# Linear attention, then two MLPs, on one core: the order of the first eight steps and of the loads ahead of them

## The chip, the cores and the metric

The kernel runs on 1 core of one Trainium2 chip. The metric is device microseconds of one execution, the median of the runs. A core has TensorE (PE), VectorE (DVE), ScalarE (ACT), GpSimd (POOL) and SyncE (SP), which issues nearly all of the DMAs here. PE, DVE and ACT work through their instructions in the order in which they were written out; so does SP with its DMAs.

## The reference

```python
# attention without softmax: 8 batches, 8 heads, 576 tokens, 64 per head
kv = np.einsum('bhsd,bhse->bhde', k, v)
out = np.einsum('bhsd,bhde->bhse', q, kv)
rms = np.sqrt(np.mean(out * out, axis=-1, keepdims=True) + 1e-06)
attn = out / rms * g_norm
x = attn.transpose(0, 2, 1, 3).reshape(4608, 512)
# first MLP, 512 -> 2048 -> 512
h = x @ w_in
x = (h * np.cos(h)) @ w_out
# second MLP, 512 -> 1024 -> 1024 -> 512
a = x @ w1
b = x @ w2
out = (a * b @ w3) @ w_out2
```

## The kernel before

**Tiles and stages.** The 4608 tokens are cut in nine blocks of 512 for the first MLP, and its 2048 inner columns in sixteen pieces m of 128. One step is one pair (block, m). A step makes h (12 matmuls of 128x512: four chunks of the 512 inputs, each as three products of a high and a low half, `three`, L756), then g = h cos h, and two steps later adds g times a piece of w_out to the four banks of x2 (`emit_w`, L786, 12 matmuls). The eight steps 0 to 7 (`HM` is 8) are block 0 with m 0 to 7; then block 1 runs with all sixteen m, and only then the second half of block 0. The second MLP (L990) takes the rest of the span.

**Words.** The weights arrive as 64-bit words and are converted on the chip, one tile of 128x512 at a time (`Chunk`, L118). A conversion is one pass of ACT (L141) and four of DVE (L142 to L149); then `put` makes the high half on ACT (L112) and the low half on DVE (L114). Tiles i0, i1, ... are w_in of piece 0, 1, ..., tiles u0, u1, ... are w_out; they come in the order i0 i1 i2 u0 i3 u1 and so on. `prefetch(n)` issues loads up to tile n, `begin` starts one conversion, `each` makes one further DVE pass on the conversions in hand.

**Attention.** A batch has two units (halves of its tokens) and four pairs of heads p. For a pair: 20 small matmuls make kv (`emit_kv`, L264; the last four read `kvrest`, the tail of the tokens), ACT copies the two 64x64 blocks (`copy_kv`, L459), PE multiplies q of the two units by them (`emit_whole`, L465), ACT squares the result (`emit_square`, L475) and keeps it times the norm's weight (`emit_keep`, L481), and PE sums the squares (`emit_sums`, L484, six small matmuls a unit). When all pairs are summed, `norms` (L493) makes 1/rms in eleven short DVE instructions, PE spreads it over the rows (`emit_rows`, L497), and DVE multiplies the kept result by it. `split_x` (L736) makes the high and the low half of x for a block.

**The first batches.** Block 0 is units 0 and 1, all of batch 0, made in `first_batch` (L511) ahead of step 0. Units 2 and 3 (batch 1) are made inside the steps 0 to 7, in `first_steps` (L571). From step 8 on a scheduler orders the work; in `first_batch` and `first_steps` the order on PE, DVE and ACT is the order of the code. `load_first` (L407) gives the order of SP's loads in the head. A load goes out when one of eight earlier ones has landed, and for a word tile also when its buffer has been converted.

**What ties the engines.** h has two PSUM banks: h of a step needs the product with the cosine (L642) of the step two back. g has two buffers: ACT's high half of g (L112) waits until x2 of two steps back has read its buffer. The banks "pa" are two; kv of a pair, the outputs of units 2 and 3 and their spread rows take turns in them. In the steps' output banks the squares' sums have a corner of their own, so a pair's q matmul must wait until ACT has kept the pair before.

**One step of `first_steps` before.** In the code's order: h of step n; squares and sums of pair p = n - 2; x2 of step n - 2; ACT's r and DVE's first u (L632, L633, called the phase here); DVE passes; the sine (L637); product (L642); split of g; keep of pair p; q matmuls of pair n - 1; more passes, then `put`. Norms come at the end of step 5, rows in steps 6 and 7.

Of the kernel before, what the change touches and what calls it, by code (L numbers as in the profile page):

```python
# [33 lines left out]
def kernel(  # L34
# [18 lines left out]
    nc = tc.nc  # L53
# [353 lines left out]
    def load_first():  # L407
# [32 lines left out]
        kv(0, 1, nc.sync)  # L440
        prefetch(1)
        kv(0, 2, nc.sync)
        qs(0, 2, nc.sync)
        prefetch(2)
        kv(0, 3, nc.sync)
        qs(0, 3, nc.sync)
        prefetch(6)
        rest(1, nc.sync)
        kv(1, 0, nc.sync)
        kv(1, 1, nc.sync)  # L450
        prefetch(8)
        for p in range(NPAIR):
            if p >= 2:
                kv(1, p, nc.sync)
            qs(1, p, nc.sync)

    whole = []
# [53 lines left out]
    def first_batch(spread, x, y, t):  # L511

        sums = ps_h.tile([P, 512], F32, tag="h", name="ms_first")
        units = range(NHALF)
        count = [1, 1, 2, 2]

        def pieces(n):
            made = [c.convert() for c in chunks[state["conv"]:state["conv"] + n]]
# [13 lines left out]
        for p in range(NPAIR):  # L532
            for u in units:
                emit_whole(u, p, ps_acc.tile(
                    [P, 512], F32, tag=f"acc{(2 * p + u) % 4}", name=f"out_{u}_{p}"
                )[:, 0:HALF])
            for u in units:
                emit_square(u, p)
            if p == 0:
                made = pieces(count[0])  # L540
            rest_of(made)
            if p > 0:
                put(count[p - 1])
            if p + 1 < NPAIR:
                emit_kv(0, p + 1)
                copy_kv(p + 1)
            if p == 0:
                nc.scalar.activation(gneg, gneg, AF.Copy, scale=-1.0)
            for u in units:
                emit_sums(u, p, sums, fresh=True)  # L550
            for u in units:
                emit_keep(u, p)
            if p + 1 < NPAIR:
                made = pieces(count[p + 1])
        for p in range(2):
            emit_kv(1, p)
        norms(sums, x, y, t)
        put(count[-1])
        for p in range(2):
            copy_kv(p)  # L560
        for p in range(NPAIR + 1):
            if p < NPAIR:
                for u in units:
                    ps = ps_acc.tile(
                        [P, 512], F32, tag=f"acc{(2 * p + u) % 4}", name=f"spread_{u}_{p}"
                    )
                    mm = emit_rows(u, p, ps, y, spread)
            if p > 0:
                split_x(0, p - 1)

    def first_steps(spread, x, y, t):  # L571
# [29 lines left out]

        prefetch(min(state["put"] + 8, n_first))
        pair = [begin(), begin()]
        for n in range(HM):
            p = n - 2
            last = n == HM - 1
            emit_h(n)
            if n == 1:
                for k in (2, 3):
                    emit_kv(1, k)  # L610
                    copy_kv(k)
                for v in units:
                    out_bank(v, 0)
            if 0 <= p < NPAIR:
                for v in units:
                    emit_square(v, p)
                sums = banks[units[0]][:, HALF:HALF + NR]
                for v in units:
                    emit_sums(v, p, sums)
            if n == NPAIR + 2:  # L620
                rows(0)
            if n >= 2:
                emit_w(n - 2)
            if n == 0:
                for _ in range(3):
                    each()
            if last:
                scale(1)
                rows(2)
# [8 lines left out]
            if last:  # L638
                for c in range(2):
                    split_x(1, c)  # L640
            new = [begin()] if n < HM - 2 else []
            nc.vector.tensor_tensor(u, u, h_ps.pop(n), ALU.mult)  # L642
            if n > 0:
                each()
            if last:
                scale(2)
                rows(3)
            g_hl[n] = m1.tile([P, 2, TB], F32R, tag="g", bufs=2, name=f"g_{n}")
            since.extend([h_last.pop(n), *split(g_hl[n], u, nc.vector)])
            new += [begin()] if n < HM - 2 else []  # L650
            if 0 <= p < NPAIR:
                for v in units:
                    emit_keep(v, p)
            if 1 < n <= NPAIR:
                for v in units:
                    out_bank(v, n - 1)
            if n == NPAIR + 2:
                scale(0)
                rows(1)
# [4 lines left out]
            if n == NPAIR + 1:  # L664
                norms(sums, x, y, t)
        split_x(1, 2)
        scale(3)
        made = split_x(1, 3)
# [714 lines left out]
```

## Time and profile before

| | us |
|---|---|
| median of 3 runs | 1538.41 |
| lowest, highest | 1533.98, 1540.04 |
| the profiled execution | 1537.59 |
| its span, first to last instruction | 1535.5 |
| PE busy in the span | 1490.5 |
| DVE, ACT, POOL busy | 866.8, 675.0, 349.3 |

The profile's times are those of the profiled execution, counted from its first instruction. A matmul's busy time overlaps that of the next one, so a stretch in which PE is fully busy says that there was always a matmul under way, not how fast it went; the granted clock beside it says whether the clock was at its upper level (1.00) or the lower one (0.50). A wait is shown in brackets behind the instruction that waited, with what ended it.

### The profile page before, as it was taken

Reading aid. Unit: us, or ns where it says so; the run is one execution under the profiler, and the core shown is the slowest. Engines: PE = TensorE matmul, PEld = TensorE weight load, DVE = VectorE, ACT = ScalarE, POOL = GpSimd, SP = SyncE. Lnnn points to the kernel's source line nnn. Section 1 sums busy time; section 2 is a strip of 40 time slices with the busy share of each in tenths; the row PEclk is TensorE's granted clock in tenths of the full one; section 3 lists DMA queues with packets and bytes.
Section 4 is the critical chain, followed back from the end, with each engine's and each line's share of the span. In section 5 each row is a group of like instructions: output and inputs, shape, how many; then the busy total and the mean of one; then the engine's idle time right before and its main releaser. Section 6 shows DMA issues by size and latency. Waiting matters only on the chain.

```text
span 1535.5 us, 20577 instructions
## 1 busy us (share of the span) xinstructions
PE 1490.5 (97%) x7728; PEld 1273.7 (83%) x7728; DVE 866.8 (56%) x1558; ACT 675.0 (44%) x1356; POOL 349.3 (23%) x278
## 2 busy tenths in 40 slices
PE   5879999999999999999999998999999999999998
PEld 4667888888788887888888887999999988999997
DVE  4777854456465665656555436755545546445543
ACT  4545654444445454444534335444433334333331
POOL 0000011010010111101102005455344237344330
PEclk7989999999999999999999999999999999999999
DMA  9325231433424435244222106122112313233312
GB/s 361 126 69 156 69 90 41 148 88 110 126 78 132 130 100 149 85 123 132 85 74 80 41 8 226 42 69 69 53 58 83 110 48 110 74 112 124 124 62 76
DMA packets 81299, 155.02 MB, mean 101 GB/s; under 512 B 11232, under 2 KB 36944, under 8 KB 81200
## 3 DMA queue, kind: packets, MB, share of 16 engines
q1 hardware_dynamic: 80224, 152.08, 30.4%
q8 instruction: 60, 0.98, 0.3%
q0 software_dynamic: 272, 1.05, 0.2%
q10 hardware_dynamic: 704, 0.59, 0.1%
q14 instruction: 39, 0.32, 0.1%
HBM read 112.57 MB, written 41.12 MB: 100 GB/s over the span
## 4 chain that ended last, share of the span: by engine, by line
PE 91%; DMA 3%; DVE 2%; ACT 1%; POOL 1%; issue 1%; SPq 0%; ACTq 0%; DVEq 0%
PE X L990 13%; PE x L757 9%; PE x L758 9%; PE h L757 9%; PE x L759 8%; PE h L758 8%; PE h L759 8%; PE V L990 6%; PE o L758 4%; PE o L757 4%; PE o L759 4%; PE Y L990 3%; PE kv L277 2%; DMA q<-in_qt_dram 1%; DMA u_w<-in_w1pair_dram 1%
## 5 line engine op out<-in xcount | busy, mean ns | idle before, releaser
L990 PE MATMUL X<-xc,w 128*128 128x384 f32 x1152 | 226.3, 337 | 4.5 <-DVE wchl L114 2.3
L758 PE MATMUL x<-g,w_out 128*128 128x512 f32 x576 | 225.3, 391 | 0.0
L759 PE MATMUL x<-g,w_out 128*128 128x512 f32 x576 | 224.7, 390 | 0.0
L757 PE MATMUL x<-g,w_out 128*128 128x512 f32 x576 | 223.2, 394 | 0.0
L776 DVE SCALAR_TENSOR_TENSOR u<-h,r 128x512 f32<-128x512 f32 x136 | 93.9, 691 | 216.7 <-ACT r L774 212.0
L757 PE MATMUL h<-x,w_in 128*128 128x512 f32 x544 | 215.6, 397 | 0.0
L990 PEld LDWEIGHTS X<-xc,w 128*128 128x128 f32 x1152 | 204.3, 189 | 12.0 <-ACT s L998 3.2
L758 PE MATMUL h<-x,w_in 128*128 128x512 f32 x544 | 213.2, 392 | 0.2 <-DVE x L114 0.2
L759 PE MATMUL h<-x,w_in 128*128 128x512 f32 x544 | 212.9, 391 | 0.0
L114 POOL TENSOR_TENSOR xc<-x2r,xc 128x768 fp32r<-128x768 f32 x70 | 135.1, 1940 | 228.6 <-ACT xc L112 228.6
L774 ACT ACTIVATE r<-h 128x512 int32<-128x512 f32 x136 | 81.1, 597 | 212.7 <-PE h L759 203.2
L114 POOL TENSOR_TENSOR qhl<-q,qhl 128x288 fp32r<-128x288 f32 x48 | 40.1, 835 | 469.9 <-ACT qhl L112 469.9
L112 ACT ACTIVATE g<-u 128x512 fp32r<-128x512 f32 x144 | 91.0, 632 | 126.9 <-DVE u L781 84.5
L114 DVE TENSOR_TENSOR g<-u,g 128x512 fp32r<-128x512 f32 x144 | 102.9, 714 | 63.1 <-ACT g L112 62.9
L998 ACT ACTIVATE s<-X 128x384 f32<-128x384 f32 x144 | 66.6, 488 | 152.5 <-PE X L990 151.9
L757 PEld LDWEIGHTS x<-g,w_out 128*128 128x128 f32 x576 | 108.5, 188 | 23.3 <-issue 0.2
L759 PEld LDWEIGHTS x<-g,w_out 128*128 128x128 f32 x576 | 108.4, 188 | 22.7
L758 PEld LDWEIGHTS x<-g,w_out 128*128 128x128 f32 x576 | 108.6, 189 | 22.0
L757 PEld LDWEIGHTS h<-x,w_in 128*128 128x128 f32 x544 | 102.8, 189 | 25.4 <-DVE u L781 3.3
L759 PEld LDWEIGHTS h<-x,w_in 128*128 128x128 f32 x544 | 102.7, 189 | 21.4
L758 PEld LDWEIGHTS h<-x,w_in 128*128 128x128 f32 x544 | 102.7, 189 | 21.0 <-DVE x L114 0.6
L781 DVE TENSOR_TENSOR u<-u,h 128x512 f32<-128x512 f32 x136 | 93.0, 684 | 47.4 <-ACT u L780 47.3
(177 smaller groups left out, 2479.2 us busy)
## 6 DMA issues: line engine op xcount, KB each, us to landing
x2r<-x_all SPq DMA_DIRECT2D x44, 384.0 KB
kvraw<-in_kv_main_dram SPq DMA_DIRECT2D x32, 512.0 KB
x_all<-x2s SPq DMA_DIRECT2D x36, 256.0 KB
part<-o SPq DMA_DIRECT2D x36, 256.0 KB
part<-part SPq DMA_DIRECT2D x36, 256.0 KB
out_dram<-part SPq DMA_DIRECT2D x36, 256.0 KB
i_w<-in_w1pair_dram SPq DMA_DIRECT2D x16, 512.0 KB
u_w<-in_w1pair_dram SPq DMA_DIRECT2D x16, 512.0 KB
```

The lines of the kernel that those rows point to most:

```text
L112: hi = nc.scalar.activation(dst[:, 0], src, AF.Copy)
L114: lo = lo_engine.tensor_tensor(dst[:, 1], src, f32(dst[:, 0]), ALU.subtract)
L277: nc.tensor.matmul(ps[d], k[:, d], v[:, d], start=fresh and i == 0, stop=i == NC, skip_group_check=True,)
L757: nc.tensor.matmul(ps, w[0], x[0], start=first, stop=False)
L758: nc.tensor.matmul(ps, w[0], x[1], start=False, stop=False)
L759: return nc.tensor.matmul(ps, w[1], x[0], start=False, stop=last).ins
L774: nc.scalar.activation(r, h_ps[n], AF.Identity, bias=0.25, scale=INV_2PI)
L776: nc.vector.scalar_tensor_tensor(u, h_ps[n], INV_2PI, r, ALU.mult, ALU.subtract)
L781: nc.vector.tensor_tensor(u, u, h_ps.pop(n), ALU.mult)
L990: nc.tensor.matmul(ps, w[:, self.i, a, k], x[:, b, k], start=first and k == 0 and n == 0, stop=last and k == 1 and n == 2, skip_group_chec ...
L998: copied.append(nc.scalar.activation(s, ps, AF.Copy).ins)
```

## The change

In `load_first` the word tiles come sooner: tile 1 ahead of q of pair 2, tile 2 behind it, tile 3 behind the fourth kv, all eight ahead of the second batch's tail; and the second batch's four kv loads stand ahead of its q loads in the code. (On SP the second batch's loads come out in nearly the same order as before, its tail of the tokens still last but for one q load.)

In `first_batch` the conversions are taken 1, 1, 1, 1 and 2 at a time, so that the fourth tile is converted behind the third. The kv matmuls of the second batch's pairs 0 and 1 and their copies are no longer there.

On PE, at the end of `first_batch`, there stood before (ms_first is the sum of squares, kv_1 the second batch, spread the rows of 1/rms):

```order
L488 MATMUL ms_first_168<-sel_86,sq_1_3_312 96x2 x3
L277 MATMUL kv_1_0_336<-kvraw_1_0_146 64x64 x8
L277 MATMUL kv_1_0_336<-kvrest_1_144 64x64 x2
L277 MATMUL kv_1_1_347<-kvraw_1_1_148 64x64 x8
L277 MATMUL kv_1_1_347<-kvrest_1_144 64x64 x2
L501 MATMUL spread_0_0_379<-rs_first_99 64x96 x6
L501 MATMUL spread_1_0_387<-rs_first_99 64x96 x6
```

and now:

```order
L487 MATMUL ms_first_168<-sel_86,sq_0_3_310 96x2 x3
L487 MATMUL ms_first_168<-sel_86,sq_1_3_312 96x2 x3
L500 MATMUL spread_0_0_353<-rs_first_99 64x96 x6
L500 MATMUL spread_1_0_361<-rs_first_99 64x96 x6
L500 MATMUL spread_0_1_369<-rs_first_99 64x96 x6
```

The kv groups have gone behind h of step 1, where those of pairs 2 and 3 already were; the copies of pairs 2 and 3 stay behind the first `put` of the steps.

In `first_steps` a step now runs as: x2 of step n - 2; h of step n + 1; r, phase, passes, sine; squares of pair n - 1; product, split of g; sums and keep of pair n - 1; q matmuls of pair n; last passes and `put`. So h of a step is made a step sooner, and the attention pairs run one step sooner too. On ACT, step 2 stood so before (sq squares, o keep, r and u the step's phase and sine, i and u with _f word tiles):

```order
L479 ACTIVATE sq_2_0_610<-out_2_561 128x288
L479 ACTIVATE sq_3_0_613<-out_3_563 128x288
L632 ACTIVATE r_2_637<-h_2_596 128x512
L637 ACTIVATE u_2_638<-u_2_638 128x512
L141 ACTIVATE i7_f_646<-i7_w_470 128x512
L112 ACTIVATE g_2_651<-u_2_638 128x512
L141 ACTIVATE u5_f_654<-u5_w_472 128x512
L482 ACTIVATE o_2_609<-out_2_561,gneg_87 128x288
L482 ACTIVATE o_3_612<-out_3_563,gneg_87 128x288
```

and stands so now:

```order
L627 ACTIVATE r_2_654<-h_2_565 128x512
L632 ACTIVATE u_2_655<-u_2_655 128x512
L478 ACTIVATE sq_2_1_663<-out_2_561 128x288
L478 ACTIVATE sq_3_1_665<-out_3_563 128x288
L141 ACTIVATE i7_f_667<-i7_w_444 128x512
L112 ACTIVATE g_2_672<-u_2_655 128x512
L481 ACTIVATE o_2_587<-out_2_561,gneg_87 128x288
L481 ACTIVATE o_3_590<-out_3_563,gneg_87 128x288
L141 ACTIVATE u5_f_685<-u5_w_446 128x512
```

The squares are of pair 1 instead of pair 0 and stand behind the sine; the keep stands ahead of the second word tile's pass.

The norms of units 2 and 3 stay in step 5, now ahead of the low halves of that step's `put`, with the rows of pair 0 directly behind them; rows of pair 1 stand between x2 of step 4 and h of step 7, rows 2 behind h of step 7, rows 3 behind x2 of step 5. Step 6 converts one word tile instead of two; the other one (u8) is converted ahead of step 8's phase. From step 8 on the scheduler makes another order. On PE the end of h of step 9 and x2 of step 7 were apart:

```order
L757 MATMUL h_9_1101<-x_1_1013,w_in1_278 128x512
L758 MATMUL h_9_1101<-x_1_1013,w_in1_278 128x512
L759 MATMUL h_9_1101<-x_1_1013,w_in1_278 128x512
L757 MATMUL x2_0_0_621<-g_7_1043,w_out7_873 128x512
L758 MATMUL x2_0_0_621<-g_7_1043,w_out7_873 128x512
L759 MATMUL x2_0_0_621<-g_7_1043,w_out7_873 128x512
```

and are now mixed with h of step 8:

```order
L766 MATMUL x2_0_0_625<-g_7_1032,w_out7_909 128x512
L766 MATMUL x2_0_1_629<-g_7_1032,w_out7_909 128x512
L766 MATMUL x2_0_2_633<-g_7_1032,w_out7_909 128x512
L766 MATMUL h_8_1068<-x_1_1018,w_in0_234 128x512
L766 MATMUL h_9_1101<-x_1_1018,w_in1_272 128x512
L767 MATMUL x2_0_0_625<-g_7_1032,w_out7_909 128x512
L768 MATMUL x2_0_0_625<-g_7_1032,w_out7_909 128x512
L767 MATMUL h_8_1068<-x_1_1018,w_in0_234 128x512
```

The second halves of h of both steps moved back, in among x2 of step 7. Further back PE has the same instructions in the same order but for some small moves in steps 10 to 18.

The diff, cut to its core:

```diff
         kv(0, 2, nc.sync)
+        prefetch(2)
         qs(0, 2, nc.sync)
-        prefetch(2)
+        prefetch(3)
         kv(0, 3, nc.sync)
+        prefetch(4)
         qs(0, 3, nc.sync)
-        prefetch(6)
+        prefetch(8)
         rest(1, nc.sync)
...
-        count = [1, 1, 2, 2]
+        count = [1, 1, 1, 1, 2]
...
+            if p == 2:
+                rest_of(pieces(count[3]))
             if p + 1 < NPAIR:
-                made = pieces(count[p + 1])
-        for p in range(2):
-            emit_kv(1, p)
+                made = pieces(count[p + 1 if p < 2 else 4])
         norms(sums, x, y, t)
         put(count[-1])
-        for p in range(2):
-            copy_kv(p)
...
+        emit_h(0)
+        emit_h(1)
         for n in range(HM):
-            p = n - 2
-            last = n == HM - 1
-            emit_h(n)
+            p = n - 1
+            begins = 2 if n < 5 else 1 if n == 5 else 0
...
             if n >= 2:
                 emit_w(n - 2)
+            if n == 6:
+                scale(0)
+                rows(1)
+            if 1 <= n < HM - 1:
+                emit_h(n + 1)
...
+            if 0 <= p < NPAIR:
+                for v in units:
+                    emit_square(v, p)
...
+            if n == 0:
+                for k in range(NPAIR):
+                    emit_kv(1, k)
+                    if k < 2:
+                        copy_kv(k)
             if 0 <= p < NPAIR:
+                sums = banks[units[0]][:, HALF:HALF + NR]
+                for v in units:
+                    emit_sums(v, p, sums)
                 for v in units:
                     emit_keep(v, p)
+                if p + 1 < NPAIR:
+                    for v in units:
+                        out_bank(v, p + 1)
...
+            if n == 5:
+                norms(sums, x, y, t)
+                rows(0)
             put(len(pair))
+            if n == 0:
+                for k in (2, 3):
+                    copy_kv(k)
+            if n == 6:
+                scale(1)
+                rows(2)
```

## Rows read from the trace of the kernel before

**Rows 1.** The page, engines: busy us, share of the span, instructions.

```profile
PE 1490.5 (97%) x7728; PEld 1273.7 (83%) x7728; DVE 866.8 (56%) x1558; ACT 675.0 (44%) x1356; POOL 349.3 (23%) x278
```

**Rows 2.** Busy time by stretch: length; PE, PEld, DVE, ACT, POOL; clock; DMA share; GB/s.

```profile
27.50:38.00 10.50, 1.84 (x26) 1.51 (x24) 5.05 (x16) 1.61 (x4) 0.00 (x0) 0.50 1.04 396
...
56.00:99.00 43.00, 34.84 (x170) 27.35 (x168) 34.79 (x65) 26.49 (x52) 0.00 (x0) 0.96 0.32 112
...
125.00:180.00 55.00, 55.00 (x271) 44.45 (x270) 45.08 (x83) 30.43 (x55) 0.81 (x1) 1.00 0.37 115
180.00:1535.00 1355.00, 1344.53 (x6801) 1156.37 (x6799) 737.90 (x1293) 583.30 (x1165) 343.85 (x260) 1.00 0.29 93
```

**Rows 3.** The chain that ended last, from 16 us: start, us, what.

```profile
27.93 8.20 DMA kvrest<-in_kv_tail_dram
```

**Rows 4.** Timeline, 27 to 44 us: start, us, instruction, [idle before <- what ended it].

```profile
29.14 0.20 DVE L494 TENSOR_SCALAR rs_first<-ms_first 96x48 f32<-96x48 f32 x1
...
36.17 0.48 PE L277 MATMUL kv<-kvrest 64*64 64x64 f32 x4 [8.66 <-DMA kvrest<-in_kv_tail_dram]
...
38.03 6.11 PE L501 MATMUL spread<-rs_first 96*64 96x96 f32 x96
```

**Rows 5.** Timeline, 8 to 19 us: loads on SP, a word tile's first passes.

```profile
8.79 0.33 SPq L413 DMA_DIRECT2D kvraw<-in_kv_main_dram  x1
...
10.60 0.33 SPq L132 DMA_DIRECT2D i_w<-in_w1pair_dram  x1
...
18.20 0.67 ACT L141 ACTIVATE i_f<-i_w 128x512 f32<-128x512 f32 x1 [0.39 <-DMA i_w<-in_w1pair_dram]
18.90 0.43 DVE L142 TENSOR_SCALAR i_f<-i_f 128x512 f32<-128x512 f32 x1 [0.48 <-ACT i_f L141]
```

**Rows 6.** Timeline, 50 to 57 us: from kv of the second batch to step 1.

```profile
50.27 0.69 PE L277 MATMUL kv<-kvraw 128*64 128x64 f32 x16
...
55.05 1.66 PE L467 MATMUL out<-q,rs_first 128*128 128x288 f32 x4 [2.95 <-ACT rs_first L463]
...
56.12 0.69 DVE L633 SCALAR_TENSOR_TENSOR u<-h,r 128x512 f32<-128x512 f32 x1 [0.74 <-ACT r L632]
```

**Rows 7.** Timeline, 62 to 74 us: step 2 on DVE, ACT and PE, step 3's phase.

```profile
63.54 0.69 DVE L633 SCALAR_TENSOR_TENSOR u<-h,r 128x512 f32<-128x512 f32 x1 [0.39 <-ACT r L632]
...
70.14 0.69 DVE L114 TENSOR_TENSOR w_out<-u_f,w_out 128x512 fp32r<-128x512 f32 x1
73.17 0.69 DVE L633 SCALAR_TENSOR_TENSOR u<-h,r 128x512 f32<-128x512 f32 x1 [2.34 <-ACT r L632]
...
66.88 0.63 ACT L112 ACTIVATE g<-u 128x512 fp32r<-128x512 f32 x1 [1.42 <-PE x L759]
...
67.96 0.87 ACT L482 ACTIVATE o<-out,gneg 128x288 f32<-128x288 f32 x2
...
68.50 1.24 PE L467 MATMUL out<-q,rs_first 128*128 128x288 f32 x4 [1.66 <-ACT o L482]
72.34 1.10 PE L488 MATMUL out<-sel,sq 128*96 128x2 f32 x12
```

**Rows 8.** Timeline, 99 to 125 us: norms of units 2 and 3, rows, step 8.

```profile
99.14 0.20 DVE L494 TENSOR_SCALAR rs_first<-out 96x48 f32<-96x48 f32 x1
...
101.85 2.19 PE L501 MATMUL spread<-rs_first 96*64 96x96 f32 x24 [3.90 <-DVE rs_first L370]
...
110.26 2.15 PE L501 MATMUL spread<-rs_first 96*64 96x96 f32 x24 [1.90 <-DVE o L600]
...
120.99 1.21 PE L501 MATMUL spread<-rs_first 96*64 96x96 f32 x24 [1.13 <-DVE o L600]
122.13 0.50 PE L757 MATMUL x<-g,w_out 128*128 128x512 f32 x1
...
124.98 0.39 PE L757 MATMUL h<-x,w_in 128*128 128x512 f32 x1
```

**Rows 9.** Timeline, 115 to 150 us: step 8's phase on DVE.

```profile
128.82 0.69 DVE L776 SCALAR_TENSOR_TENSOR u<-h,r 128x512 f32<-128x512 f32 x1 [3.89 <-ACT r L774]
```

More of the change, by code (lines that the diff above doesn't have):

```diff
@@ L442, in load_first @@
         kv(0, 2, nc.sync)
+        prefetch(2)
         qs(0, 2, nc.sync)
-        prefetch(2)
+        prefetch(3)
         kv(0, 3, nc.sync)
+        prefetch(4)
         qs(0, 3, nc.sync)
-        prefetch(6)
+        prefetch(8)
         rest(1, nc.sync)
-        kv(1, 0, nc.sync)
-        kv(1, 1, nc.sync)
-        prefetch(8)
         for p in range(NPAIR):
-            if p >= 2:
-                kv(1, p, nc.sync)
+            kv(1, p, nc.sync)
+        for p in range(NPAIR):
             qs(1, p, nc.sync)
@@ L542, in first_batch @@
             if p > 0:
-                put(count[p - 1])
+                put(count[p - 1] if p < 3 else 2)
             if p + 1 < NPAIR:
@@ L566, in first_batch @@
                     )
-                    mm = emit_rows(u, p, ps, y, spread)
+                    emit_rows(u, p, ps, y, spread)
             if p > 0:
@@ L603, in first_steps @@
         pair = [begin(), begin()]
+        emit_h(0)
+        emit_h(1)
         for n in range(HM):
-            p = n - 2
-            last = n == HM - 1
-            emit_h(n)
+            p = n - 1
+            begins = 2 if n < 5 else 1 if n == 5 else 0
+            new = []
             if n == 1:
-                for k in (2, 3):
-                    emit_kv(1, k)
-                    copy_kv(k)
                 for v in units:
                     out_bank(v, 0)
[L614 to L621, printed above, removed]
             if n >= 2:
                 emit_w(n - 2)
+            if n == 6:
[3 more added lines that the diff above has]
+                emit_h(n + 1)
             if n == 0:
@@ L626, in first_steps @@
                     each()
-            if last:
-                scale(1)
-                rows(2)
+            if n == HM - 1:
+                scale(2)
+                rows(3)
             r = stage([P, TB], I32, f"r_{n}")
@@ L637, in first_steps @@
             nc.scalar.activation(u, u, AF.Sin, bias=HALF_PI, scale=TWO_PI)
-            if last:
+            if n == HM - 1:
                 for c in range(2):
                     split_x(1, c)
-            new = [begin()] if n < HM - 2 else []
+            if 0 <= p < NPAIR:
+                for v in units:
+                    emit_square(v, p)
+            if begins > 0:
+                new.append(begin())
             nc.vector.tensor_tensor(u, u, h_ps.pop(n), ALU.mult)
@@ L644, in first_steps @@
                 each()
-            if last:
-                scale(2)
-                rows(3)
             g_hl[n] = m1.tile([P, 2, TB], F32R, tag="g", bufs=2, name=f"g_{n}")
             since.extend([h_last.pop(n), *split(g_hl[n], u, nc.vector)])
-            new += [begin()] if n < HM - 2 else []
+            if n == 0:
[3 more added lines that the diff above has]
+                        copy_kv(k)
             if 0 <= p < NPAIR:
+                sums = banks[units[0]][:, HALF:HALF + NR]
+                for v in units:
+                    emit_sums(v, p, sums)
                 for v in units:
                     emit_keep(v, p)
[L654 to L659, printed above, removed]
+                if p + 1 < NPAIR:
+                    for v in units:
+                        out_bank(v, p + 1)
+            if begins > 1:
+                new.append(begin())
             each()
+            if n == 5:
+                norms(sums, x, y, t)
+                rows(0)
             put(len(pair))
+            if n == 0:
[4 more added lines that the diff above has]
+                rows(2)
             pair = new
             prefetch(min(state["put"] + 8, n_first))
-            if n == NPAIR + 1:
-                norms(sums, x, y, t)
         split_x(1, 2)
```

## The prediction

> **What bounds the kernel now.** The page's table of engines was read first: TensorE (PE) is busy for 97% of the span [rows 1]. So a change pays only where it takes idle or slow time out of PE. The busy time by stretch shows where that is [rows 2]: from 125 to 180 us PE is busy 55.00 of 55, and from 180 to 1535 us it is busy 1344.53 of 1355. From 125 us on the kernel is PE's own work, at granted clock 1.00, and it starts when the first eight steps are over. Ahead of that PE is idle for some 34 us: 8.66 of the 10.5 from 27.5 to 38, and 8.2 of the 43 from 56 to 99, where VectorE (DVE) is busy 34.79 and so doesn't fill the time either. The change touches only this head. The mark for it is the first matmul of step 8, at 124.98 us [rows 8]: what it moves forward, the end moves forward, as long as nothing behind it becomes later than PE.
>
> Three things hold the head. First, one load: PE waits 8.66 us for the tail of the second batch's kv, which lands at 36.1, 8.2 us after it was issued [rows 3, 4]. The norms of the first batch start at 29.14 and need none of it, but their spread matmuls stand behind it, at 38.03. Second, the steps: step 2's phase on DVE starts at 63.54 and the next at 73.17, 9.63 us later, though DVE's last instruction of the step starts at 70.14. It then waits 2.34 for ScalarE's r, which waits for h on PE. ScalarE (ACT) in its turn waits 1.42 for PE's x, because g has two buffers, and PE waits 1.66 for ACT's copy of the attention output [rows 7]. So the three engines hand one step round, one after the other. Third, the norms of units 2 and 3: PE waits 3.90, then 1.90 and 1.13 for rows and scales [rows 8].
>
> **The first batch.** The four kv matmul groups go behind the second h. Spread then follows the norms. From the norms' first instruction to the first spread matmul it takes 2.71 us in the second batch (99.14 to 101.85 [rows 8]), so from 29.14 the spread would start at 31.85, not 38.03: 6.2 us. There is some more. DVE converts words without a break from 18.90 to 29.14, and that run begins with a word tile for which ACT had waited until 18.20 [rows 5]. This tile was issued at 10.60. In the new queue it takes the place of the load at 8.79, 1.8 us sooner. Of these 1.8 I take 0.8, since the fourth tile's first pass is now behind a copy on ACT. What it passes on SP's queue goes back: the fourth kv load by that one slot, q of pair 3 by two word tiles. Their readers on PE stand behind the squares' sums, so I cost that at nothing; uncovered it would take back some 0.4. First term: **7.0**, ends 5.8 (no sooner word, a late kv load) and 8.0 (all 1.8).
>
> The Trainium skill, DMA: Bandwidth & Descriptors, section Specifications, gives about 358 GB/s as what one core gets from HBM. The trace moved 396 in 27.5 to 38 [rows 2], so the measurement decides; by the page's figure the words of the first 16 us would land about a tenth later, and the sum below would be an estimated 1.6 us smaller.
>
> Where does the kv wait go? The tail lands at 36.1 as before, since it is in the same place in the queue behind the same bytes. Its first reader is now behind two h, which end some 7 us sooner than the 50.27 at which the later kv groups began, at 43.3. The cover is 7 us. Next late are ACT's copies of kv: out of pair 0 waited 2.95 for them [rows 6], and still does, for the last two copies stay behind the two weight halves.
>
> **Steps 0 to 5.** The stretch from the phase of step 1 (56.12 [rows 6]) to the norms (99.14 [rows 8]) is 43.0 us. For the new one, DVE's work of a step: from 63.54 to 70.14 plus a spacing of 0.60 it is 7.2, of which 0.2 is a wait for ACT: 7.0 a step [rows 7]. PE's work of a step: twelve matmuls of x2 take 2.85 (122.13 to 124.98 [rows 8]), twelve of h about as much less their start-up, 2.75; out 1.24, sums 1.10 [rows 7]; 7.8 with little overlap taken off. The new order lets the two run beside each other: h of step n+1 is made while ACT and DVE are in step n, and x of step n-2 stands ahead of it, so that g's buffer is free early. The loop that could close across engines is out, x, g, keep, next out: 1.24 + 2.85 + 0.63 + 0.87 for two copies [rows 7], 5.6, under PE's 7.8. PE enters this with a lead of one h, steps 0 and 1 have less for it to do, and step 4 has no out. Laid out from the new order, h of step 5 ends about 1.5 us before DVE has finished step 4. So DVE is the later one: four steps of 7.0, then 5.6 from the phase of step 5 to the norms, 33.6. Two more kv copies go ahead of ACT's weight halves in step 0; 0.2 of them lies outside the idle time there. Second term: 43.0 - 33.6 - 0.2 = **9.2**. Ends: 10.2 if DVE's waits inside the step go too, 6.0 if PE's 7.8 sets each step.
>
> **Norms to step 8.** Today 25.84 (99.14 to 124.98). The norms still stop PE: h of step 6 ends, laid out, 0.7 before DVE gets to them, so PE again waits some 3 us, and the slow clock behind that wait stays. But rows now stand ahead of h and x, with scales made a phase sooner, so the waits of 1.90 and 1.13 go: 3.0. Behind the 1.90 the spread took 2.15 where the same 24 matmuls took 1.21 elsewhere; x2 behind the norms took from 104.04 to 108.36, 4.3 against 2.85 [rows 8]. Without the second wait 1.6 of such slow time can go; I take half. Third term: **3.8**. Ends: 2.0 (a scale is late again) and 7.1 (no slow time at all, 1.6 + 2.5).
>
> **Step 8 on.** One word conversion moves from step 6 to before step 8's phase: five DVE passes of 0.54 (19 fill the run from 18.90 to 29.14), 2.7. DVE was idle 3.89 there [rows 9], which covers it. But the new order also mixes h of steps 8 and 9 with x2 of step 7 on PE, so r of step 8 comes near the end of the 36 matmuls, and h of step 10 waits for its bank: phase, sine, product, some 0.8 us beyond the kv group that covers it. Fourth term: **-0.8**, ends 0 and -2.7 (all of the conversion uncovered).
>
> **The sum** is 7.0 + 9.2 + 3.8 - 0.8 = 19.2 us. The profiled execution took 1537.59 us, 2.1 more than its span; it becomes 1518.4. It lies 0.8 under the median of the runs, so **1519** is the forecast. With all lower ends 11.1 us are left (1528), with all upper ends 25.3 (1514).
>
> **Rivals.** *A, the steps keep their period.* If each engine's hand-over is late by more than the 2.2 us between the loop's 5.6 and PE's 7.8, the steps stay near 9.6. For it: ACT sits in all loops and now does squares and copies inside its g chain. Against it: in a step ACT has 5.9 us of work (26.49 of 43, times 9.6 [rows 2]) and waits the rest. Then 7.0 + 3.8 - 0.8 = 10 us remain: 1529. *B, the head is only shifted.* From 150 us DVE runs near PE's pace; if the conversions behind step 8 become the bound, perhaps 14 of the 19 us are given back: 1533. Against it: 125 to 180 has 10 us of free DVE time [rows 2]. *C, slower.* The place is steps 1 to 7 on PE. If it ran there at 0.50, as it was granted from 27.5 to 38 [rows 2], each of the 156 matmuls from h of step 2 to x2 of step 6 would take twice its 0.23 (2.75 by twelve): 36 us more, and 1555. It decides from about 84 slow matmuls up, which use up the 19.2. Against it: the low clock followed PE's waits of 8.66, 2.95 and 3.90, and two of the three shrink or stay. *D, the clock stays up.* With shorter waits PE may not fall to 1.2 GHz in the tail at all: 3.3 us more than I counted in the third term, 1515.5. *E, the load still stops PE,* behind h, because the queue is later than now by over 7 us: the first term is lost, 1526.
>
> The Trainium skill, TensorE: Matmul & The Clock Gate, section Part 1: The HAM clock gate, calls the throttled clock the default that activity releases; by that rule D's time holds and C's doesn't, and the trace agrees so far as its low clocks all stand at PE's waits.
>
> **How the numbers follow.** Forecast 0.58, D 0.13, A 0.14, B 0.08, C 0.04, E 0.03. A measurement of this kernel can tell about 0.5%, 7.7 us, from no change: faster means under 1530.7. That holds for the forecast, D, E and most of A: 0.85. Within 0.5% are most of B and a rest of A: 0.10. Slower are C and a little of B: 0.05. The range from 1512 to 1530 leaves out B, C and about half of A.
>
> **What will show it.** Right: spread of the first batch starts near 31, the norms of the second batch near 83 (7.0 + 9.2 ahead of 99.14), the first matmul of step 8 near 105.0, PE without waits behind it but for about 1 us, and the phases of steps 2 to 5 about 7 to 8 us apart. Wrong: phases still 9 us apart (A), waits of PE between 110 and 180 (B), granted clock near 0.5 in the steps (C), or a wait for kv behind the second h (E).

## The result, and the profile after

The changed kernel takes **1521.86 us** (median of 6 runs, 1520.61 to 1523.88), the kernel before 1538.47 in the same runs: ratio 0.9898, 95% interval 0.9879 to 0.9916. That is 16.6 us less. The forecast was 1519 with a range from 1512 to 1530, so the time lies inside it and 2.9 us above the forecast. The sign and the place of the gain held. What sets the spacing of the steps, and the sizes of the terms, did not come out as forecast.

The page of the changed kernel, engines: PE's share rises from 97 to 98%, with less busy time (1484.1 us for 1490.5 [rows 1]); that fits fewer matmuls at the low clock.

```profile
PE 1484.1 (98%) x7728; PEld 1269.3 (84%) x7728; DVE 868.4 (57%) x1558; ACT 673.6 (44%) x1356; POOL 349.3 (23%) x278
```

The windows of the changed kernel (length; PE, PEld, DVE, ACT, POOL; clock; DMA share; GB/s) answer to [rows 2]. PE's work is now 6.28 us of the stretch from 27.5 to 38 instead of 1.84. From 125 to 180 it has no gap, as before.

```profile
27.50:38.00 10.50, 6.28 (x88) 6.31 (x90) 8.19 (x25) 3.16 (x7) 0.00 (x0) 0.54 1.04 396
38.00:56.00 18.00, 16.12 (x151) 12.72 (x148) 15.55 (x33) 12.95 (x30) 1.59 (x2) 1.00 0.43 155
56.00:99.00 43.00, 35.91 (x205) 29.44 (x204) 35.47 (x74) 22.35 (x45) 0.00 (x0) 0.92 0.29 98
...
125.00:180.00 55.00, 55.00 (x291) 44.38 (x289) 47.72 (x89) 31.64 (x63) 3.15 (x3) 1.00 0.37 122
```

The timeline of the changed kernel in the order of the four terms: the norms and the spread of the first batch; the first q matmuls of batch 1 and step 1's phase; one step; the norms of units 2 and 3 up to the mark (the first matmul of step 8); and the wait behind it.

```profile
29.01 0.20 DVE L493 TENSOR_SCALAR rs_first<-ms_first 96x48 f32<-96x48 f32 x1
31.73 6.83 PE L500 MATMUL spread<-rs_first 96*64 96x96 f32 x96 [6.69 <-DVE rs_first L370]
...
49.20 1.24 PE L466 MATMUL out<-q,rs_first 128*128 128x288 f32 x4 [0.90 <-ACT rs_first L462]
50.28 0.69 DVE L628 SCALAR_TENSOR_TENSOR u<-h,r 128x512 f32<-128x512 f32 x1 [0.84 <-ACT r L627]
...
57.38 0.69 DVE L628 SCALAR_TENSOR_TENSOR u<-h,r 128x512 f32<-128x512 f32 x1
61.25 1.10 PE L487 MATMUL out<-sel,sq 128*96 128x2 f32 x12
62.39 0.89 ACT L481 ACTIVATE o<-out,gneg 128x288 f32<-128x288 f32 x2 [1.66 <-PE out L487]
62.94 1.24 PE L466 MATMUL out<-q,rs_first 128*128 128x288 f32 x4 [0.59 <-ACT o L481]
64.38 0.69 DVE L114 TENSOR_TENSOR w_in<-i_f,w_in 128x512 fp32r<-128x512 f32 x1 [1.37 <-ACT w_in L112]
65.59 0.68 DVE L628 SCALAR_TENSOR_TENSOR u<-h,r 128x512 f32<-128x512 f32 x1
...
87.63 0.20 DVE L493 TENSOR_SCALAR rs_first<-out 96x48 f32<-96x48 f32 x1
90.34 2.19 PE L500 MATMUL spread<-rs_first 96*64 96x96 f32 x24 [5.91 <-DVE rs_first L370]
...
106.04 0.50 PE L766 MATMUL x<-g,w_out 128*128 128x512 f32 x1
...
108.91 0.39 PE L766 MATMUL h<-x,w_in 128*128 128x512 f32 x1
119.26 0.69 PE L277 MATMUL kv<-kvraw 128*64 128x64 f32 x16 [2.03 <-DMA kvraw<-in_kv_main_dram]
```

The spread stands at 31.73 where it stood at 38.03 [rows 4]. The phases of steps 1 to 5 are at 50.28, 57.38, 65.59, 73.86 and 82.08: 7.1 and then three times 8.2 to 8.3 apart; before, the last three spacings were 9.6 to 9.4. The mark has moved from 124.98 [rows 8] to 108.91, by 16.07.

To compare executions, one more mark is needed. The first loads of an execution vary: the first batch's norms start between 27.45 and 31.73 in the profiles of this case whose first batch is the changed kernel's. From the phase of step 16 to that of the last step, on the other hand, no two of the profiles differ by more than 0.4 us. So the table counts from the norms of the first batch (the row of DVE at 29.14 in [rows 4]) to the phase of step 16:

| us | norms 1 to phase 1 | to norms of units 2, 3 | to the mark | to phase 16 | sum |
|---|---|---|---|---|---|
| before | 26.98 | 43.02 | 25.84 | 46.84 | 142.68 |
| changed | 21.27 | 37.35 | 21.28 | 48.97 | 128.87 |
| gain | 5.71 | 5.67 | 4.56 | -2.13 | 13.81 |

The other 1.7 us of the profiled difference in span (15.5) lie outside: 0.1 in the start, 0.3 between steps 16 and 19, 1.3 behind the last step's phase, in the second MLP. That last part took from 614.5 to 617.1 us across the profiles, also between executions of unchanged order. In the profile of the kernel before, the clock fell in it, in that of the changed kernel it did not (see the last section), so I don't count it to the change.

### The profile page after: what moved, and what is told of

Same layout as the page of the kernel before. It is cut to its first block, busy times and chain, and to the rows that moved or that the text cites. A ratio compares the mean times of both kernels' runs of the same rounds, so it can differ in the third digit from the quotient of the medians.

```text
span 1520.0 us, 20574 instructions
## 1 busy us (share of the span) xinstructions
PE 1484.1 (98%) x7728; PEld 1269.3 (84%) x7728; DVE 868.4 (57%) x1558; ACT 673.6 (44%) x1356; POOL 349.3 (23%) x278
## 4 chain that ended last, share of the span: by engine, by line
PE 92%; DVE 3%; ACT 1%; DMA 1%; issue 1%; POOL 1%; SPq 0%; DVEq 0%; ACTq 0%
PE X L999 13%; PE x L766 9%; PE h L766 9%; PE x L767 8%; PE x L768 8%; PE h L767 8%; PE h L768 8%; PE V L999 6%; PE o L767 4%; PE o L766 4%; PE o L768 4%; PE Y L999 3%; PE kv L277 2%; PE spread L500 1%; PE out L466 1%
```

## The experiments

Each is an edit of the changed kernel but for the second, which is one of the kernel before.

**kv groups back.** The first two kv groups of batch 1 stand ahead of the norms again.

```diff
+        for p in range(2):
+            emit_kv(1, p)
         norms(sums, x, y, t)
         put(count[-1])
+        for p in range(2):
+            copy_kv(p)
...
             if n == 0:
-                for k in range(NPAIR):
+                for k in (2, 3):
                     emit_kv(1, k)
-                    if k < 2:
-                        copy_kv(k)
```

> The changed kernel with one part undone: the kv groups of pairs 0 and 1 of the second batch stand ahead of the first batch's norms again, as before the change; the loads and the steps stay changed. Theory: the load's wait was worth 6.3 us by itself (the spread moved from 38.03 to 31.73). PE should wait some 8 us for that load again, the spread should start at 38 to 39 (the load now stands behind two more word tiles), the granted clock should be low around it, and the norms of the second batch and the first matmul of step 8 should move back by about 6 from 87.63 and 108.91, to 94 and 115; time about 1528. Rival: the steps have slack behind the wait (words or loads limit them), and then less than 3 us come back: time 1522 to 1525, norms of the second batch under 91.

Measured: 1532.28 us (ratio to before 0.9957, 0.9942 to 0.9971), 10.4 more than the changed kernel, where I expected 6. Against the kernel before in the same runs (1539.43) it is 7.2 less, so 9.5 of the 16.6 are gone. Its timeline, PE and step 1's and step 2's phases:

```profile
35.83 0.48 PE L277 MATMUL kv<-kvrest 64*64 64x64 f32 x4 [8.44 <-DMA kvrest<-in_kv_tail_dram]
55.20 2.29 PE L466 MATMUL out<-q,rs_first 128*128 128x288 f32 x4 [2.97 <-ACT rs_first L462]
57.72 0.63 PE L769 MATMUL h<-x,w_in 128*128 128x512 f32 x1
...
56.28 0.69 DVE L632 SCALAR_TENSOR_TENSOR u<-h,r 128x512 f32<-128x512 f32 x1 [0.74 <-ACT r L631]
65.94 0.69 DVE L632 SCALAR_TENSOR_TENSOR u<-h,r 128x512 f32<-128x512 f32 x1
```

The load's wait is back (8.44) and makes step 1's phase 6.1 later, as the theory asks for. But more follows: PE waits 2.97 for the copies of kv, and behind that it runs at the low clock (0.63 us for a matmul that takes 0.39 elsewhere), so that step 2's phase comes 9.66 after step 1's instead of 7.10. From norms 1 to the norms of units 2 and 3 it takes 67.28 us, 8.66 more than in the changed kernel. Another 1.6 is lost behind the mark: PE's wait for the next kv load, 2.13 here and 2.03 in the changed kernel, is followed by the low clock in this execution and not in that one (last section).

**kv groups alone.** The kernel before, with only this part of the change.

```diff
-        for p in range(2):
-            emit_kv(1, p)
         norms(sums, x, y, t)
...
-        for p in range(2):
-            copy_kv(p)
...
             if n == 1:
-                for k in (2, 3):
+                for k in range(NPAIR):
                     emit_kv(1, k)
```

> The kernel before with one part of the change alone: the four kv groups of the second batch behind the second h; the loads, the steps and the tail stay as they were. Theory: the spread starts at 31.9 where it was 38.03, the phase of step 1 comes about 6 us sooner than 56.12, the steps keep their spacing of 9.6, and all else moves with it: first matmul of step 8 at 119 instead of 124.98, time 1532.4 (6 us less). Rival: the old order needs the new one to pass the gain on (kv groups and their copies now stand in step 1, with two more copies of each in ACT's chain): phase of step 1 less than 4 us sooner and time 1535 or more.

Measured: 1536.57 us (ratio 0.9982, 0.9973 to 0.9992), 2.9 less than before, not 6. In its profile nothing at all is left: norms 1 to phase 16 takes 142.55, before 142.68. (The profiled execution, 1539.43 us, is the slowest of the ten.) Its timeline (PE, the phases of steps 1 to 3, then PE and ACT in step 2) and one window, with the columns as above, show where it goes.

```profile
49.64 0.72 PE L277 MATMUL kv<-kvraw 128*64 128x64 f32 x16 [2.95 <-ACT rs_first L463]
...
53.38 0.69 DVE L629 SCALAR_TENSOR_TENSOR u<-h,r 128x512 f32<-128x512 f32 x1 [3.40 <-ACT r L628]
60.81 0.69 DVE L629 SCALAR_TENSOR_TENSOR u<-h,r 128x512 f32<-128x512 f32 x1 [0.40 <-ACT r L628]
73.49 0.69 DVE L629 SCALAR_TENSOR_TENSOR u<-h,r 128x512 f32<-128x512 f32 x1 [2.35 <-ACT r L628]
...
60.04 1.79 PE L488 MATMUL out<-sel,sq 128*96 128x2 f32 x12 [1.61 <-ACT sq L479]
66.53 0.63 PE L755 MATMUL x<-g,w_out 128*128 128x512 f32 x1
67.19 0.63 ACT L112 ACTIVATE g<-u 128x512 fp32r<-128x512 f32 x1 [4.43 <-PE x L755]
```

The window from 64 to 70 us, at granted clock 0.73:

```profile
64.00:70.00 6.00, 4.33 (x13) 2.92 (x12) 2.69 (x6) 2.79 (x6) 0.00 (x0) 0.73 0.00 0
```

Step 2's phase is still 2.73 sooner than before (60.81 for 63.54 [rows 7]); counted from the first norms, which start at 30.02 here and at 29.14 before, it is 3.6 sooner. Then x2 of step 0 runs wholly at the low clock, with 0.63 a matmul to its last at 66.53. ACT waits 4.43 for it because g has two buffers, and step 3's phase stands at 73.49, where it was 73.17 [rows 7], only 0.6 sooner from the norms. This low clock follows a wait of 1.61 for the squares. The kernel before waits 2.13 at the same place and runs on at the full clock:

```profile
62.77 1.18 PE L488 MATMUL out<-sel,sq 128*96 128x2 f32 x12 [2.13 <-ACT sq L479]
```

Steps and kv groups need each other. In the one profile of each, the kv groups alone give 0.1 us up to phase 16 (142.68 to 142.55), and the change without them gives 3.1 (to 139.64); together it is 13.8. The medians give 2.9 and 7.2 of 16.6. So what the parts owe to each other is 10.6 us by the profiles and 6.5 by the medians. The change without the kv groups also holds the changed tail and word loads.

**The old tail.** Rows and scales of units 2 and 3 in the old order.

```diff
+            if n == 6:
+                rows(0)
             if n >= 2:
                 emit_w(n - 2)
-            if n == 6:
-                scale(0)
-                rows(1)
...
             if n == HM - 1:
-                scale(2)
-                rows(3)
+                scale(1)
+                rows(2)
...
+            if n == HM - 1:
+                scale(2)
+                rows(3)
             g_hl[n] = m1.tile([P, 2, TB], F32R, tag="g", bufs=2, name=f"g_{n}")
...
                 norms(sums, x, y, t)
-                rows(0)
...
             if n == 6:
-                scale(1)
-                rows(2)
+                scale(0)
+                rows(1)
```

> The changed kernel with the old order of rows and scales behind the norms of the second batch: rows 0 at the head of step 6, scale 0 and rows 1 at its end, and so on, each scale one place later than in the change. Theory: the tail's gain of 4.6 us (norms to the first matmul of step 8 in 21.28 instead of 25.84) comes from this order: PE gets waits of 1 to 2 us for the scales again, with slower matmuls behind them, and the stretch is 24 to 26; time 1525 to 1527. Rival: the stretch is short because x and h were moved, not the rows (x of two steps back and h of the next step give PE work there in any case): under 22.5, time 1522 to 1523.

Measured: 1524.06 us (0.9889 to 0.9918). PE waits for scales again, for less than before:

```profile
100.82 1.21 PE L500 MATMUL spread<-rs_first 96*64 96x96 f32 x24 [1.18 <-DVE o L597]
104.94 1.21 PE L500 MATMUL spread<-rs_first 96*64 96x96 f32 x24
106.75 1.21 PE L500 MATMUL spread<-rs_first 96*64 96x96 f32 x24 [0.59 <-DVE o L597]
...
110.76 0.39 PE L767 MATMUL h<-x,w_in 128*128 128x512 f32 x1
```

Norms to mark is 22.96 at most (110.76 is the second matmul of its group), between the two theories: of the tail's 4.56 us, 1.7 come from the order of rows and scales, and the other 2.9, by subtraction, from x and h having moved. And even the 1.7 do not last: the wait of 2.03 behind the mark isn't there in this kernel, and at phase 16 it stands at 128.39, 0.5 ahead of the changed kernel.

**Words late.** The old order of loads and of conversions in the first batch.

```diff
         kv(0, 2, nc.sync)
-        prefetch(2)
         qs(0, 2, nc.sync)
-        prefetch(3)
+        prefetch(2)
         kv(0, 3, nc.sync)
-        prefetch(4)
         qs(0, 3, nc.sync)
-        prefetch(8)
+        prefetch(6)
         rest(1, nc.sync)
...
-        count = [1, 1, 1, 1, 2]
+        count = [1, 1, 2, 2]
```

> The changed kernel with the old order of loads and conversions in the first batch: word tiles two to four behind q and kv, conversions one, one, two, two. The steps and the kv groups stay changed. Theory: the sooner words bought nothing, since the norms of the first batch start at 29.01 where they started at 29.14: norms at 29.1, spread at 31.9, first matmul of step 8 within 0.5 of 108.91, time within 1 us of 1521.9. Rival: they bought the 0.8 us that the prediction took: norms at 29.8 or later and time 1522.7 or more.

Measured: 1523.3 us (1521.93 to 1525.18), 16.1 less than the kernel before in the same runs, where the changed kernel was 16.6 less. The norms start at 29.44 instead of 29.01, inside the scatter of the first loads (27.45 to 31.73), so what the sooner words are worth in the first batch can't be told: 0.4 or nothing. At phase 16 this kernel is 2.1 us later than the changed one (130.98). 1.5 of it lie behind the mark, and the trace shows why. PE waits for the same kv load and for the same time as in the changed kernel, but here the low clock follows: from 121 to 124 us the granted clock is 0.50, where it is 1.00 in the changed kernel, and the 16 kv matmuls take 0.84 us instead of 0.69.

```profile
120.32 0.84 PE L277 MATMUL kv<-kvraw 128*64 128x64 f32 x16 [2.04 <-DMA kvraw<-in_kv_main_dram]
```

The order of the words isn't shown to be the cause of that: other profiles differ at this place too (last section).

**Keep first.** ScalarE's copies of the attention output stand ahead of the sums of squares.

```diff
                 for v in units:
-                    emit_sums(v, p, sums)
-                for v in units:
                     emit_keep(v, p)
+                for v in units:
+                    emit_sums(v, p, sums)
```

> The changed kernel with two lines exchanged in the steps: ScalarE's copies of the attention output (keep) stand ahead of the sums of squares on TensorE, which are written into the same bank. Theory: the steps are 8.24 us apart because keep waits 1.7 for the sums, which stand behind x and h on PE, and PE then waits 0.59 for keep and DVE 1.4 for ACT's weight half. Without it the phases of steps 2 to 5 are 7.6 to 7.8 apart (PE's own work: x 2.85, h 2.75, sums 1.1, out 1.24), ACT's wait for sums and DVE's 1.4 are gone, the norms start near 85.5 instead of 87.63, and the time is about 2 us less, 1520. Rival P: PE's work with its start-ups is 8.2 by itself; the phases stay 8.2 apart and only the place of the waits changes. Rival S: sums now wait for keep on PE, more than 0.6 a step; phases over 8.4 apart and the time 1 to 3 us more.

Measured: 1517.0 us (1513.72 to 1526.17; ratio 0.9861, 0.9839 to 0.9884), 4.9 less than the changed kernel, where I expected 2. Phases, norms, a keep, and PE at the rows:

```profile
57.07 0.68 DVE L628 SCALAR_TENSOR_TENSOR u<-h,r 128x512 f32<-128x512 f32 x1
64.01 0.68 DVE L628 SCALAR_TENSOR_TENSOR u<-h,r 128x512 f32<-128x512 f32 x1
70.94 0.68 DVE L628 SCALAR_TENSOR_TENSOR u<-h,r 128x512 f32<-128x512 f32 x1
77.88 0.68 DVE L628 SCALAR_TENSOR_TENSOR u<-h,r 128x512 f32<-128x512 f32 x1
83.43 0.20 DVE L493 TENSOR_SCALAR rs_first<-out 96x48 f32<-96x48 f32 x1
...
67.26 0.88 ACT L481 ACTIVATE o<-out,gneg 128x288 f32<-128x288 f32 x2
...
86.14 1.21 PE L500 MATMUL spread<-rs_first 96*64 96x96 f32 x24 [3.00 <-DVE rs_first L370]
...
102.47 0.39 PE L766 MATMUL h<-x,w_in 128*128 128x512 f32 x1
```

The steps are 6.94 us apart, which is DVE's own work: its rows stand without waits. Phase 1 to the norms is 33.31, where the changed kernel takes 37.35 and the prediction had 33.6. PE makes its steps in 7.5 and uses up its lead, so it waits only 3.00 at the norms, and the 24 matmuls behind it take 1.21, not 2.19: the clock stayed at 1.00. Norms to mark falls to 19.04. Both rivals that I had set against this, a PE that needs 8.2 by itself and sums that wait for keep, fall.

**The word conversion back in step 6.**

```diff
-            begins = 2 if n < 5 else 1 if n == 5 else 0
+            begins = 2 if n < 6 else 0
```

> The changed kernel with the word conversion that the change moved from step 6 to before step 8's phase put back into step 6. Theory: behind step 8 PE waits 2.03 for a kv load because this load stands on SP's queue behind a word tile, and that tile's buffer is free only when this conversion is done, at 112.6. With the conversion in step 6 the load is issued by 107 and the wait is gone; the five passes (2.7 us) now lie on DVE in the tail, so the first matmul of step 8 comes 0.5 to 2 us later than 108.91. Together 0 to 1.5 us less, time 1520.4 to 1522. Rival: the wait is due to the transfer itself or its place behind the copies of x, not to the word tile: it stays at 2 us and the time is 0.5 to 2 us more.

Measured: 1522.02 us (1519.86 to 1524.94). The wait for the kv load is gone, so the theory on its cause holds. Behind the kv group PE now waits 0.97 for DVE's product before h of step 10, and the mark comes 0.28 later after the norms. At phase 16 this kernel is 0.9 ahead (127.95): less than the runs can resolve.

**Filling the wait at the norms.** x of step 4 and h of step 7 ahead of the rows.

```diff
+            if 1 <= n < HM - 1:
+                emit_h(n + 1)
             if n == 6:
+                rows(0)
                 scale(0)
                 rows(1)
-            if 1 <= n < HM - 1:
-                emit_h(n + 1)
...
                 norms(sums, x, y, t)
-                rows(0)
```

> The changed kernel with x of step 4 and h of step 7 ahead of the rows on PE in step 6, so that PE has work while DVE makes the norms of units 2 and 3 (where it waits 5.91 us now). Theory: behind the norms DVE sets the end of the tail (its instructions from the norms to the last part of x add to 17.2 of the 20 us it takes), so of PE's 5.6 us of work that is moved only 1.5 to 2.7 show: PE's wait at the norms falls to under 1 us, the granted clock stays at 1.00, but PE waits for scales or for x later; first matmul of step 8 at 106.2 to 107.4, time 1519.2 to 1520.4. Rival P: PE alone sets the tail, and the whole 5.6 show: first matmul of step 8 at 103.5, time 1516. Rival N: nothing shows, since the last scale waits for a chain of DVE and ACT that doesn't move: 108.9, time 1522.

Measured: 1522.61 us (1520.58 to 1524.66), no difference that shows; 1.5 to 2.7 was expected, with the clock at 1.00. PE at the rows:

```profile
92.77 1.21 PE L500 MATMUL spread<-rs_first 96*64 96x96 f32 x24 [0.47 <-DVE rs_first L370]
94.24 1.21 PE L500 MATMUL spread<-rs_first 96*64 96x96 f32 x24 [0.27 <-DVE o L597]
100.40 2.19 PE L500 MATMUL spread<-rs_first 96*64 96x96 f32 x24 [4.95 <-DVE o L597]
```

PE's wait of 5.91 becomes 0.47, and a new one of 4.95 stands at the third rows, which need a scale that DVE makes at the end of step 6; the low clock moves with the wait. Of 5.6 us of work moved, 1.0 shows at the mark (norms to mark 20.31): DVE's order sets the tail. At phase 16 its profile is 2.0 ahead (126.88): 1.0 from the mark, and 0.9 because PE's wait for the kv load behind it is 1.15 here, not 2.03.

**All three.**

> The changed kernel with the three edits together: keep ahead of the sums, the conversion back in step 6, and x of step 4 and h of step 7 ahead of the rows. Theory: the gains add where they lie in different stretches: steps 2 us, tail 1.5 to 2.7 less the conversion's passes on DVE (0.5 to 2), the kv wait 2: time 1516 to 1519. Rival: the tail is DVE's, and the conversion there costs what the fill gives; then 1519 to 1520, no better than keep ahead of the sums with the fill.

Measured: 1519.14 us (1518.6 to 1521.86), no gain on keep first. The steps are those of keep first (33.31), but norms to mark is 24.20, for PE waits 6.58 for that same scale:

```profile
97.56 2.19 PE L500 MATMUL spread<-rs_first 96*64 96x96 f32 x24 [6.58 <-DVE o L597]
```

It is the fill that harms here, where the wait was 3.00 and cost no clock: the next group has keep first with the conversion and without the fill, and takes 122.18 us from norms 1 to phase 16, for 125.39 with it.

**The changed kernel, keep first, and keep first with the conversion in step 6, on one chip.**

> The changed kernel itself again, on the same chip as the two next: 1521.9 as before, first matmul of step 8 near 108.9.

> Keep ahead of the sums, once more, beside the changed kernel on one chip, since the first runs of it lay from 1513.7 to 1526.2. Theory: steps 6.94 apart, PE's wait at the norms 3.0 with no low clock behind it, first matmul of step 8 at 102.5, 6.4 us ahead of the changed kernel, and the time 5 to 6.5 us less than its time. Rival: the high clock behind the wait of 3.0 was luck of that execution; then the first matmul of step 8 is near 104.7 and the time some 4 us less.

> Keep ahead of the sums, and the conversion put back into step 6. Theory: DVE has 2.7 us more to do in the tail, where with keep first it has some 3 us of waits; the first matmul of step 8 comes 0 to 1 us later than 102.5; the kv wait of 2.1 behind step 8 is gone and 1.0 of it comes back as a wait of h of step 10 for its bank: 0 to 1 us less than keep alone. Rival: the five passes push the last scale back by their 2.7: 104 to 105 for the first matmul of step 8, and 1 to 2 us more than keep alone.

Measured: 1524.19 (1520.05 to 1528.7; ratio 0.9901), **1517.99** (1516.58 to 1520.91; 0.9864, 0.985 to 0.9878) and **1517.85** us (1517.51 to 1520.38; 0.9866, 0.9851 to 0.9882). From norms 1 to phase 16 the second profile of keep first takes 122.51 (the first took 122.53), that of the changed kernel 128.58, the third kernel 122.18. The second profile of keep first again has its rows at the norms at 1.21 behind a wait of 3.01, and the third kernel behind 3.03:

```profile
88.86 1.21 PE L500 MATMUL spread<-rs_first 96*64 96x96 f32 x24 [3.01 <-DVE rs_first L370]
```

Three profiles of three speak against luck, but don't exclude it: at other places executions with equal waits differ in their clock (last section). Exchanging two loops is worth 6 us more; with it the head gains 20.2 us on before. The conversion adds nothing that a run can tell: PE's wait for the load is replaced by one at h of step 10, in the third kernel's timeline:

```profile
113.47 0.50 PE L766 MATMUL h<-x,w_in 128*128 128x512 f32 x1 [0.98 <-DVE u L790]
```

## Why the prediction was right, and which steps failed

**Bound and mark: right.** Nearly all of the gain is idle or slow time of PE ahead of step 16, and behind it the two kernels run alike. Of the signs that the prediction named, the spread near 31 came (31.73); the norms of the second batch near 83 and the mark near 105.0 did not (87.63 and 108.91), and the phases were 7.1 and then 8.2 apart, not 7 to 8. The ends of its sum, 11.1 and 25.3, make 1527 and 1513 of the median of 1538.4, not 1528 and 1514; nothing hangs on that.

**The first batch: 7.0 predicted, 5.7 to 5.8 measured.** The move of the kv groups gave 6.3 at the spread, as worked out (6.2). Of the step "Of these 1.8 I take 0.8" no run shows anything: the norms came 0.13 sooner in the two executions compared, and the first loads scatter by more. The step that failed is that the term ends at the start of the spread. The spread starts at the low clock in both kernels, but before, the granted clock was 0.50 from 38 to 42 us and 1.00 behind, 4 us into the spread; now it is 0.50 from 32 to 37, more than 5 us into it. So the spread takes 6.83 us for 6.11 [rows 4]. The tail of kv no longer stops anything, and the wait of out for kv's copies, which I left at 2.95, shrank to 0.90.

**Steps 0 to 5: 9.2 predicted, 5.7 measured.** This is the largest miss: 3.5 of the 5.4 us by which the four terms (19.2) are above what the table shows (13.8). That the time is off by only 2.9 is in part luck: 1.7 us of the profiled gain lie outside the four terms, and the medians are 0.9 further apart than the two profiled executions. The failing sentence is "The loop that could close across engines is out, x, g, keep, next out ... 5.6, under PE's 7.8." The sums of squares are written into the bank of unit 2's output, and stand in the code ahead of keep, so keep waits for them (1.66 above). On PE they stand behind x and h. The loop is out 1.24, x and h 5.3 together, sums 1.10, hand-over to ACT and back 0.59: from one out at 62.94 to the next 8.26. That this was the cause is shown by keep first: without the hand-over the stretch takes 33.31, and the prediction's DVE bound (7.0 a step, 33.6) is what is left. The bound was right, and the changed kernel did not reach it. The Trainium skill, PSUM — Partial Sum Buffer, section PSUM bank collisions raise a hardware error, says to guard PSUM by bank and group of partitions, not by address; the trace agrees, since keep reads other columns of the bank than the sums write and yet waits 1.66 for them. Read against the order of the code, that rule gives the loop away.

**Norms to step 8: 3.8 predicted, 4.56 measured.** The waits for scales are gone, as predicted. PE's wait at the norms is 5.91, not "some 3", with the low clock behind it as forecast; the longer wait followed from the slower steps, for with keep first it is 3.00. The part put down to rows and scales is smaller than I held (1.7 by the old tail); moving x and h did the rest, by subtraction.

**Step 8 on: -0.8 predicted, -2.13 measured at phase 16,** inside the ends 0 and -2.7, for another reason. The conversion that moved behind the mark did not cost its passes on DVE. It holds a word tile's buffer, that tile's load waits on SP, and kvraw stands behind it. SP's timeline of the changed kernel, step 7 to step 9:

```profile
106.20 0.33 SPq L132 DMA_DIRECT2D u_w<-in_w1pair_dram  x1
112.66 0.33 SPq L132 DMA_DIRECT2D i_w<-in_w1pair_dram  x1
113.04 0.42 SPq L247 DMA_DIRECT2D kvrest<-in_kv_tail_dram  x1
113.51 0.43 SPq L258 DMA_DIRECT2D kvraw<-in_kv_main_dram  x1
```

I had costed the moved instruction on its engine and not on the queue behind it. The bank wait of h of step 10 that I had named (0.8) is real, 0.97 where the load's wait is gone; the two are alternatives, and the longer one counts. The size of this term also holds some luck: where the low clock followed the load's wait (kv groups back, words late), 1.5 to 1.6 more was lost by phase 16.

**Rivals.** A fell as a number, for the steps went from 9.6 to 8.2; its mechanism, a hand-over through ACT that sets the step, is what held them at 8.2. B fell: nothing but the 2.1 is given back. C fell too, but its mechanism exists in the two experiments with half of the change: in the one profile of each, the low clock in one step took 2.6 us (kv groups back) and 3.1 (kv groups alone). D fell for the changed kernel, where the low clock follows the wait at the norms. Keep first shows the mechanism named for D: behind a shorter wait its tail runs at full clock and is 2.2 us shorter. The other 4.0 of its gain are the steps. E fell: no wait for the tail of kv.

One reading behind C and D was wrong. The prediction has the low clock follow PE's wait of 8.66, and stand at PE's waits only. In the kernel before, the granted clock was 0.50 already ahead of that wait, from 22.0 to 27.5 us, while PE was busy for all of the 5.50 us; there the trace does not agree.

## What to carry to other kernels

Follow each hand-over through the buffers, not only through the data: two results in one PSUM bank, or two loads in one queue, are a dependency, and the loop that it closes can set the period. When two edits shorten the same chain, price them together, for a wait that only one of them removes can bring a slow clock that takes the gain back. Where executions scatter by more than the effect, compare stretches between two marks of the trace.

## What the runs showed of the hardware

The length of PE's wait alone does not tell whether the clock falls. Behind a wait of 3.00, 3.01 or 3.03 us at the norms (keep first, twice, and with the conversion) the rows ran at full clock, 1.21 for 24 matmuls; behind 3.90 [rows 8], 4.95, 5.91 and 6.58 they took 2.19. But behind 2.95 to 2.97 at the kv copies the clock fell (0.63 a matmul), and so it did behind 1.61 at the sums, where the kernel before kept it up behind 2.13.

Executions differ even at one place. At the kv load behind step 8, PE waited 2.03, 2.10, 2.11 and 2.14 us in the profiles of the changed kernel and of keep first (two of each), and the clock stayed at 1.00; it fell to 0.50 behind 2.04 (words late) and 2.13 (kv groups back). At the first twelve matmuls X of the second MLP all thirteen profiles show a wait of 2.2 to 2.3 us. In eight of them the twelve took 2.35 to 2.38 us, in the other five 2.98 to 3.91, at the low clock. The kernel before and the changed one, at this place:

```profile
956.44 3.89 PE L990 MATMUL X<-xc,w 128*128 128x384 f32 x12 [2.26 <-DVE wchl L114]
942.44 2.35 PE L999 MATMUL X<-xc,w 128*128 128x384 f32 x12 [2.25 <-DVE wchl L114]
```

So one profile shows what one execution got. A difference of 1.5 us behind a wait of this length, in a single profile, is not yet one between two kernels. What decides was not tested.
